# Moving a rarely used branch to the end of a planned three-stage kernel, with its FFN weights split in place and its planner's numbers renewed

## The chip, the core and the metric

The kernel runs on one core of a Trainium2 chip, in one launch. The metric is the device time of that launch in microseconds; the median of several runs counts. A core has five engines that each run their own list of instructions in order: TensorE (PE, with its weight loads PEld), VectorE (DVE), ScalarE (ACT), GpSimd (POOL) and SyncE (SP). They wait for one another by semaphores. DMAs are issued from the queues of SP, ACT and POOL. An instruction that waits holds up everything behind it on its engine.

## What is computed

Softcap attention, then a feed-forward network with x*sigmoid(1.702x), then a top-1 mixture of eight experts:

```python
scores = cap * tanh(scale * q @ k.T / cap)          # B=4, H=12, S=448, D=64, cap=30
attn   = softmax(scores) @ v
x = attn.transpose(0, 2, 1, 3).reshape(1792, 768)
h = x @ w_in;  x = (h * sigmoid(1.702 * h)) @ w_out  # 768 -> 2048 -> 768
e = argmax(x @ w_gate);  gate = softmax(x @ w_gate)[e];  eom = sigmoid(x @ w_output_gate)[e]
out = gate * eom * (relu(x @ w1[e]) @ w2[e])         # 8 experts, 768 -> 1024 -> 768
```

All is fp32 to the outside. Inside, a factor is split into a high part that TensorE's f32r type holds and the rest (`hi` and `lo`), and a product is made of up to three f32r matmuls: hi·hi, hi·lo, lo·hi. Where that is cheaper, one fp32 matmul is used instead.

## The kernel before

**Attention.** Each batch `b` has 12 heads of 4 chunks of 112 queries. A chunk runs `scores` (two f32r matmuls, L620-621), `tanh` (ACT, L625), `exp` (ACT, L629), then for most heads `p_hi` and `p_lo` (a rounding through `rnd_any`, L471 on ACT or L475 on DVE, and a subtraction through `rest_any`, L479; both write the tile `hl`) and `pv` (three f32r matmuls, L648-650). The first `NPVF` = 12 heads, all of batch 0, skip the split: `pv_f` (L642) is one fp32 matmul. After a pair of heads the result is copied out (`u_cp`), its sums go through a chain of small POOL DMAs (`s_ld`, `s_st`, `r_ld`; names `sm`, `rs`, `r`) and a reciprocal on DVE, and the pair is scaled into `x32` and split into `xh` and `xl`.

**Large caps.** The exponential needs no maximum while the cap is at most 40. For larger caps `wide_attention` (L245) computes attention anew in a plain loop. The test on `wide` stands at L441-443, ahead of everything planned: every engine loads the value and branches. If it ran, each pair of heads takes its `x32` from it, by a DMA on POOL's queue under a condition (`x_wide`, L704-706, `x<-xgen`), 24 in all. The condition is false here, but the instruction stands in POOL's order, and `x_hi` waits for it.

**FFN.** Eight halves (batch by half of 2048) in the order (0,0), (1,0), (1,1), (0,1), (2,0), (2,1), (3,0), (3,1). A half has 14 units of weights: 8 of `w_in` with 18 matmuls each and 6 of `w_out` with 24 (`quantum`, L958-960, tile `fps`). For the first half of each kind the weights come from the input, are put together from two words and stored to `wsp`. Later, `ld` (L766) loads a unit from `wsp` to `wf`, `hi` rounds it to the first half of tile `w` and `lo` subtracts into the second. `wf` has `WFR` = 2 buffers, `w` has `WFB` = 4. After the second half of a batch `route(b)` computes expert and place of each token; its last step are four indirect scatters into `tab` on POOL (L1087), each of which waits for the one before.

**Experts.** 21 slots of up to 128 tokens, with loads under a condition (`w_load`, L1300), splits (`w_split`, tiles `mw` and `w`), `l1` (L1391) and `l2` (L1441).

**What sets the order.** Nothing is left to a scheduler of the compiler. Class `Plan` takes tasks with a cost for each engine that may run them, a due time and the buffers they take (`Ring`), simulates them and emits the instructions of each engine in the order in which its list put them. Due times come from constants by stage (`W1`, `AO1`, `CV0`, `SLOT`, ...) less a lead by name (`LEAD`). A transfer costs `bytes / DMAR` on SP's queue and lands `DMAL` later. A task that takes a ring's buffer waits in the plan until the users of the buffer `n` places back are done, and, in `Plan.run` (L174-175), until the first user of the buffer just before it in the ring is done too:

```python
if not r.free and b.at:
    need.add(r.declared[b.at - 1].users[0])
```

For a load that second rule means that the load before has landed. On the chip the order decides, not the planner's times: a semaphore is waited for where the data needs it.

## Time and profile before

| | us |
|---|---|
| median of 3 runs | 1212.81 (1212.13 to 1213.75) |
| profiled execution, its own time | 1217.32 |
| span of its trace | 1215.7 |
| PE / DVE / ACT / POOL busy | 1113.6 / 944.9 / 824.4 / 397.4 |
| mean granted clock of TensorE | 0.976 |

The profile is one execution, 4.5 us over the median; its span lies 1.6 us under its own time. A busy PE is one with matmuls in its array, and their ends are modelled, so sums over a stretch can be compared and single ends cannot. The stretches: attention of batch 0 alone up to 70.3 us; eight FFN halves with the attention of the next batches in between up to 822.1 (the third half ends at 414.6, the first part of the fourth at 448.6, its w_out part at 505.0); experts to the end. A window row gives an engine's busy time in such a stretch, a wait row names what an engine's next instruction waited for last, a timeline row one instruction with the idle time ahead of it.

### The profile page before, as it was taken

The page shows a single profiled execution, that of the slowest core. Times are in us where ns is not written, and L with a number is a line of the kernel's source. Part 1 is how long each engine was busy: PE and PEld are TensorE (multiplying, and loading weights), DVE is VectorE, ACT ScalarE, POOL GpSimd, SP SyncE. Part 2 cuts the span into 40 slices and gives each one's busy share as a digit, 9 for nine tenths or more (in the row PEclk, how much of TensorE's full clock was granted, in tenths as well). Part 3 has the DMA queues.
Part 4 walks back from the last instruction along what each step waited for, and adds up shares of the span by engine and source line. Part 5 has one row for each costly group of instructions (what it writes and reads, how often), then busy time and mean ns, then how long its engine had stood idle before and what let it go on. Part 6 is the DMA issues. An engine that isn't in the chain of part 4 may idle for free.

```text
span 1215.7 us, 16715 instructions
## 1 busy us (share of the span) xinstructions
PE 1113.6 (92%) x5410; PEld 930.5 (77%) x5410; DVE 944.9 (78%) x1461; ACT 824.4 (68%) x1365; POOL 397.4 (33%) x313
## 2 busy tenths in 40 slices
PE   6988898699989995999999998897899999999997
PEld 2446676587777884888888887785788899899897
DVE  4789898688898464578688554558998989999885
ACT  6988798586887422357887332336588888788784
POOL 0222211131141121242132311104575565665651
PEclk9999999899999997999999999999899999999999
DMA  6974667777886574276452374713037951137720
GB/s 166 232 198 136 185 178 201 211 220 212 262 261 187 156 122 82 85 120 147 117 128 81 97 124 89 277 36 111 27 118 283 375 188 40 54 130 260 267 93 31
DMA packets 70218, 191.09 MB, mean 157 GB/s; under 512 B 11362, under 2 KB 21870, under 8 KB 70128
## 3 DMA queue, kind: packets, MB, share of 16 engines
q1 hardware_dynamic: 63440, 170.62, 49.4%
q0 software_dynamic: 6464, 19.16, 5.1%
q8 instruction: 43, 0.70, 0.2%
q14 instruction: 47, 0.39, 0.1%
q10 hardware_dynamic: 224, 0.23, 0.1%
HBM read 244.33 MB, written 28.91 MB: 225 GB/s over the span
## 4 chain that ended last, share of the span: by engine, by line
PE 38%; DMA 10%; DVE 10%; issue 6%; POOL 3%; ACT 2%; SPq 0%; POOLq 0%; DVEq 0%; ACTq 0%
PE hps L1391 8%; PE ops L1441 8%; DMA wf<-wsp 5%; PE fps L958 5%; PE fps L959 5%; PE fps L960 5%; DMA tab<-tokid,posi 2%; DVE w L479 2%; DMA xg<-x2s,gi 1%; DVE mw L479 1%; POOL mw L479 1%; POOL w L479 1%; PE gtp L1409 1%; PE xtp L1361 1%; PE tp L1033 1%
## 5 line engine op out<-in xcount | busy, mean ns | idle before, releaser
L958 PE MATMUL fps<-xh,w 128*128 128x448 f32 x384 | 144.8, 377 | 6.3 <-DVE th L982 6.3
L958 PE MATMUL fps<-gh,w 128*128 128x448 f32 x384 | 144.4, 376 | 5.6 <-ACT acc L1002 3.8
L959 PE MATMUL fps<-gl,w 128*128 128x448 f32 x384 | 142.8, 372 | 3.7 <-DVE gl L479 3.7
L959 PE MATMUL fps<-xl,w 128*128 128x448 f32 x384 | 142.9, 372 | 0.4 <-DVE xl L479 0.4
L960 PE MATMUL fps<-xh,w 128*128 128x448 f32 x384 | 142.7, 372 | 0.0
L960 PE MATMUL fps<-gh,w 128*128 128x448 f32 x384 | 142.3, 370 | 0.0
L629 ACT ACTIVATE p<-p,capa 112x448 f32<-112x448 f32 x192 | 126.4, 667 | 2.6
L479 DVE TENSOR_TENSOR w<-wf,w 128x1024 fp32r<-128x1024 f32 (+3 forms) x95 | 90.6, 959 | 41.3 <-ACT w L471 41.0
L625 ACT ACTIVATE p<-sps 112x448 f32<-112x448 f32 x184 | 97.7, 534 | 19.4 <-PE sps L621 18.0
L471 ACT ACTIVATE w<-wf 128x1024 fp32r<-128x1024 f32 (+3 forms) x75 | 63.9, 851 | 62.5 <-DMA wf<-wsp 33.5
L1441 PE MATMUL ops<-mw,gT 128*128 128x384 f32 x540 | 104.6, 344 | 0.0
L479 DVE TENSOR_TENSOR hl<-p,hl 112x448 fp32r<-112x448 f32 x134 | 95.4, 715 | 11.0 <-ACT hl L471 10.1
L479 POOL TENSOR_TENSOR w<-wf,w 128x768 fp32r<-128x768 f32 (+2 forms) x31 | 63.1, 2035 | 119.7 <-DVE w L475 63.1
L1391 PE MATMUL hps<-mw,xT 128*128 128x512 f32 x390 | 100.4, 409 | 0.0
L479 POOL TENSOR_TENSOR mw<-w1r,mw 128x1024 fp32r<-128x1024 f32 x24 | 76.3, 3193 | 64.0 <-ACT mw L471 63.9
L1441 PEld LDWEIGHTS ops<-mw,gT 128*128 128x128 f32 x540 | 95.8, 192 | 0.9
L471 ACT ACTIVATE mw<-w2r 128x768 fp32r<-128x768 f32 x90 | 75.4, 847 | 30.0 <-PE hps L1391 25.6
L620 PE MATMUL sps<-qks 128*112 128x448 f32 x184 | 79.5, 432 | 14.1 <-ACT vf L471 11.7
L479 DVE TENSOR_TENSOR mw<-w2r,mw 128x768 fp32r<-128x768 f32 x82 | 88.8, 1127 | 0.2 <-ACT mw L471 0.2
L1391 PEld LDWEIGHTS hps<-mw,xT 128*128 128x128 f32 x390 | 74.4, 194 | 16.7 <-ACT h L1404 0.2
L958 PEld LDWEIGHTS fps<-xh,w 128*128 128x128 f32 x384 | 73.5, 191 | 17.6 <-DVE th L982 7.3
L650 PE MATMUL pv<-hl,vs 112*65 112x448 f32 x144 | 55.9, 388 | 33.9 <-DVE hl L479 29.8
(232 smaller groups left out, 2711.4 us busy)
## 6 DMA issues: line engine op xcount, KB each, us to landing
w1r<-in_w_dram SPq DMA_DIRECT2D x60, 1024.0 KB
w2r<-in_w_dram SPq DMA_DIRECT2D x80, 768.0 KB
wf<-wsp SPq DMA_DIRECT2D x56, 384.0 KB
wf<-wsp SPq DMA_DIRECT2D x42, 512.0 KB
qkr<-in_qk_dram SPq DMA_DIRECT2D x95, 224.0 KB
wr<-in_w_in_dram SPq DMA_DIRECT2D x32, 384.0 KB
wr<-in_w_out_dram SPq DMA_DIRECT2D x24, 512.0 KB
x2s<-x2tok SPq DMA_DIRECT2D x4, 1358.0 KB
```

The costliest lines, as they stand in the source:

```text
L471: nc.scalar.activation(o, i, AF.Copy)
L479: e.tensor_tensor(out=o, in0=x, in1=f32(hi), op=ALU.subtract)
L620: mm(sps, lhsT=t[:, 1, sl], rhs=t[:, 0, :], start=True, stop=False)
L625: nc.scalar.activation(p, T["s", kc], AF.Tanh, scale=sct2[:CK] if qkf else 1.0)
L629: nc.scalar.activation(p, p, AF.Exp, scale=capa[:CK])
L650: mm(o, lhsT=VSh[:, 0, c, :], rhs=t[:, 1, :], start=False, stop=c == NC4 - 1)
L958: mm(fps, lhsT=wh, rhs=xh, start=c == 0, stop=False)
L959: mm(fps, lhsT=wh, rhs=xl, start=False, stop=False)
L960: mm(fps, lhsT=wl, rhs=xh, start=False, stop=c == n - 1)
L1033: nc.tensor.transpose(tp[:, j, :], T["x2", u][:, j * CK:(j + 1) * CK], ident)
L1391: mm(T["h", s][n], lhsT=x_[:, kk, :], rhs=w[:, a, n * 512:(n + 1) * 512], start=st_, stop=sp_)
L1441: mm(T["o", s][:, n, :384], lhsT=x_[:, k, :], rhs=w[:, a, n * 384:(n + 1) * 384], start=st_, stop=sp_)
```

## The change

Seven things are done at once.

1. The whole planned body becomes a function `program(ctx, general)`. It is called once with `general=False`, without a test ahead of it. After its end each engine loads `wide` and branches; for a large cap `wide_attention` and a second copy of the program, `program(True)`, which loads `x32` from `xgen`, would overwrite the output. The 24 conditional DMAs go. `exp` is scaled by `capx` = min(cap, 40), so that the first pass stays finite.
2. In the plan, the buffer just before in a ring need only have been started (`first`), not finished.
3. Transfer costs: `DMAR` 330e3 to 300e3, `DMAL` 2.6 to 4.5, POOL's issue 1.1 to 0.6, the small POOL DMAs with landings `SLAT` = (2.8, 4.6, 5.8). The scatters keep theirs, a landing of 2.0.
4. For halves after the first, `ld` loads into the second half of `w` itself, `hi` rounds it into the first and `lo` subtracts in place. `wf` is left to the first half. The load's due time goes from 4 to `WPRE` = 14 ahead.
5. `HB` (buffers of `hl`) 4 to 3, `UB` (of `u`) 2 to 3, `NPVF` 12 to 20: the first eight heads of batch 1 use one fp32 matmul too.
6. The temporary tiles of the index constants at the start share one buffer.
7. All leads and stage constants have other values. They set the order and nothing else.

```diff
-HB = 4
-UB = 2
+HB = 3
+UB = 3
-NPVF = 12
+NPVF = 20
-DMAR = 330e3
-DMAL = 2.6
+DMAR = 300e3
+DMAL = 4.5
-DMAP = 1.1
+DMAP = 0.6
+WPRE = 14.0
+SLAT = (2.8, 4.6, 5.8)
-W1 = 117.691
+W1 = 117.952
...
-                if not r.free and b.at:
-                    need.add(r.declared[b.at - 1].users[0])
+            first = {r.declared[b.at - 1].users[0] for r, b in ((b.ring, b) for b in t.takes) if not r.free and b.at} - need
+            need |= first
...
-                at = max((x.end + self.hop(x, e) for x in t.need), default=0.0)
+                at = max((x.start if x in t.first else x.end + self.hop(x, e) for x in t.need), default=0.0)
...
+    capx = const.tile([128, 1], F32, name="capx")
+    nc.vector.tensor_scalar(out=capx, in0=capa, scalar1=CAPMAX, scalar2=None, op0=ALU.min)
...
-        ti = const.tile([p, n], I32, name=name + "_i")
+        ti = const.tile([128, 32], I32, tag="iota", name=name + "_i")[:p, :n]
...
-    is_wide = nc.values_load(wide[0:1, 0:1], min_val=0, max_val=1)
-    with tc.If(is_wide == 1):
-        wide_attention(tc, nc, qk, v, sct, ncapa, ident, xg)
+    def program(ctx, general):
...
+            if general:
+                for h in range(1, H, 2):
...
+                        nc.sync.dma_start(T["x32", kp], xg[kp[0] * NPAIR + kp[1]].rearrange("a d s -> (a d) s"))
...
-                    nc.scalar.activation(p, p, AF.Exp, scale=capa[:CK])
+                        nc.scalar.activation(p, p, AF.Exp, scale=capx[:CK])
...
-            def x_wide(e, kp=kp):
-                nc.gpsimd.dma_start(T["x32", kp], xg[kp[0] * NPAIR + kp[1]].rearrange("a d s -> (a d) s"),
-                                  cond=is_wide == 1)
-            cc, l = pdma()
-            x = add(cc, s_ld, vc - STG, [xu, u_even], [ub, smb], lat=l)
+                x = add(one("POOL", DMAP), s_ld, vc - STG, [xu, u_even], [ub, smb], lat=SLAT[0])
...
-            x = add(one("POOL", 0.3), x_wide, vc - 6 * STG, [x0, x1], [x32b], lat=0.5)
+                x_split(b, kp, x1, x32b, vc, [x0])
...
-        wb, wfb = r_w.new(), r_wf.new()
+            wb = wbuf[u] = r_w.new()
+            wfb = None if j else r_wf.new()
...
-                T["wf", u] = fr.tile([128, 1024], U32, tag="wf", name="wf")
-                nc.sync.dma_start(T["wf", u][:, :m], wsp[wid][:, :m])
+                    T["w", u] = fw.tile([128, 2, 1024], F32R, tag="w", name="w")
+                    nc.sync.dma_start(T["w", u].bitcast(U32)[:, 1, :m], wsp[wid][:, :m])
...
-                rnd_any(T["w", u][:, 0, :m], f32(T["wf", u][:, :m]), e)
+                    rnd_any(T["w", u][:, 0, :m], f32(T["w", u][:, 1, :m]), e)
...
-                rest_any(T["w", u][:, 1, :m], f32(T["wf", u][:, :m]), T["w", u][:, 0, :m], e)
+                    t = T["w", u]
+                    rest_any(t[:, 1, :m], f32(t[:, 1, :m]), t[:, 0, :m], e)
...
-            x = add(c, ld, vw - 4, stored[wid], [wfb], lat=l)
-            x = add(c_rnd(m), hi, vw, [x], [wfb, wb])
-            wdone[u] = [x, add(c_rest(m), lo, vw, [x], [wfb, wb])]
+                x = add(c, ld, vw - WPRE, stored[wid], [wb], lat=l)
+                x = add(c_rnd(m), hi, vw, [x], [wb])
+                wdone[u] = [x, add(c_rest(m), lo, vw, [x], [wb])]
...
+    with ExitStack() as stack:
+        program(stack, False)
+
+    is_wide = nc.values_load(wide[0:1, 0:1], min_val=0, max_val=1)
+    with tc.If(is_wide == 1):
+        wide_attention(tc, nc, qk, v, sct, ncapa, ident, xg)
+        with ExitStack() as stack:
+            program(stack, True)
```

Lines move: what was L471, L475, L479 and L357 is L476, L480, L484 and L361 after the change; L1087 is L1099, L766 is L778, L1300 is L1312.

**POOL at route(1).** Before, from the first of the four scatters on:

```order
L1087 DMA tab<-tokid,posi 14336x1
L479 TENSOR_TENSOR w<-wf,w 128x768
L1087 DMA tab<-tokid,posi 14336x1 x3
L705 REGISTER_ALU
L705 ISA
L705 DMA x_4777<-xgen 128x448
L693 DMA r<-rs 64x896
L681 DMA sm<-u 128x1x7
L479 TENSOR_TENSOR hl<-p,hl 112x448
L705 REGISTER_ALU
```

After, the same place:

```order
L484 TENSOR_TENSOR w<-w 128x768
L1099 DMA tab<-tokid,posi 14336x1
L705 DMA rs<-sm 128x7
L1099 DMA tab<-tokid,posi 14336x1 x2
L361 TENSOR_SCALAR w<-w 128x768
L1099 DMA tab<-tokid,posi 14336x1
L484 TENSOR_TENSOR qks<-qkr,qks 128x448
L484 TENSOR_TENSOR vs<-vr,vs 112x4x64
L709 DMA r<-rs 64x896
L484 TENSOR_TENSOR w<-w 128x1024
```

The conditional transfers are gone. A rounding of a `w` (the first `w_out` unit of the fourth half) and the chain of a pair's sums now stand among the scatters.

**SP in the w_in part of the last half.** `wf` or `w` from `wsp` are FFN weights, `w1r` and `w2r` weights of the first expert slot. Before:

```order
L1300 DMA w1r_7626<-in_w_dram 128x2x1024
L766 DMA wf<-wsp 128x768
L1300 ISA
L1300 DMA w1r_7655<-in_w_dram 128x2x1024
L1300 ISA
L1300 DMA w1r_7673<-in_w_dram 128x2x1024
L766 DMA wf<-wsp 128x768
L1300 ISA
L1300 DMA w2r_7705<-in_w_dram 128x2x768
L1300 ISA
L1300 DMA w2r_7717<-in_w_dram 128x2x768
L766 DMA wf<-wsp 128x1024 x6
```

After:

```order
L1312 DMA w1r_7294<-in_w_dram 128x2x1024
L778 DMA w<-wsp 128x768
L1312 ISA
L1312 DMA w1r_7331<-in_w_dram 128x2x1024
L778 DMA w<-wsp 128x1024
L1312 ISA
L1312 DMA w1r_7366<-in_w_dram 128x2x1024
L778 DMA w<-wsp 128x1024
L1312 ISA
L1312 DMA w2r_7398<-in_w_dram 128x2x768
L778 DMA w<-wsp 128x1024
L1312 ISA
```

The loads for the experts stood two together between single FFN loads; now each is followed by one FFN load.

**DVE in the attention of batch 1**, in the heads that now use one fp32 product. Before:

```order
L479 TENSOR_TENSOR qks<-qkr,qks 128x448
L479 TENSOR_TENSOR hl<-p,hl 112x448
L475 CAST hl<-p 112x448
L479 TENSOR_TENSOR hl<-p,hl 112x448
L475 CAST hl<-p 112x448
L479 TENSOR_TENSOR hl<-p,hl 112x448
L475 CAST hl<-p 112x448
L671 COPY u<-pv 65x448
L479 TENSOR_TENSOR hl<-p,hl 112x448
```

After:

```order
L484 TENSOR_TENSOR w<-wf,w 128x384
L594 SCALAR_TENSOR_TENSOR qks<-qkr,sct,qks 64x448
L484 TENSOR_TENSOR qks<-qkr,qks 128x448
L687 COPY u<-pv 65x448
L994 SCALAR_TENSOR_TENSOR th<-th,fps 128x448
L480 CAST gh<-th 128x448
L852 TENSOR_SCALAR wg<-wr 128x384
L484 TENSOR_TENSOR gl<-th,gh 128x448
L860 SCALAR_TENSOR_TENSOR we<-we,wg 128x384
L829 SCALAR_TENSOR_TENSOR wf<-wr,we 128x384
```

The copies and subtractions into `hl` are gone; the copies of `u` stay or come to DVE, beside FFN work (`th`, `gh`, `gl`) and the making of weights (`wg`, `we`, `wf`).

## Rows read from the trace of the kernel before

**Rows 1.** Page, part 1: engine, busy us (share of the span) x instructions.
```profile
PE 1113.6 (92%) x5410; PEld 930.5 (77%) x5410; DVE 944.9 (78%) x1461; ACT 824.4 (68%) x1365; POOL 397.4 (33%) x313
```

**Rows 2.** Windows: stretch and length, busy us by engine, then granted clock, DMA share, GB/s.
```profile
0.00:70.30 70.30, 53.73 (x158) 24.86 (x159) 44.69 (x115) 54.56 (x108) 12.19 (x37) 1.00 0.73 191
70.30:329.40 259.10, 224.12 (x998) 174.07 (x997) 225.18 (x421) 206.34 (x404) 52.39 (x70) 0.95 0.71 202
...
448.60:505.00 56.40, 42.55 (x195) 34.44 (x196) 29.81 (x48) 16.03 (x28) 10.12 (x16) 0.85 0.48 80
...
461.20:478.20 17.00, 7.71 (x19) 4.45 (x20) 8.82 (x14) 5.29 (x10) 4.06 (x7) 0.50 0.48 47
...
505.00:682.50 177.50, 174.61 (x876) 149.43 (x875) 133.85 (x225) 124.28 (x225) 53.71 (x51) 1.00 0.48 114
682.50:785.60 103.10, 94.21 (x464) 84.22 (x463) 53.41 (x109) 31.82 (x53) 19.51 (x14) 0.98 0.62 156
...
895.00:1215.70 320.70, 313.13 (x1675) 282.31 (x1673) 282.27 (x272) 255.12 (x334) 174.22 (x81) 1.00 0.48 172
```

**Rows 3.** Waits of PE, 0 to 448.6 us: for what, total us, times, longest.
```profile
PE pv L650 <- DVE hl L479: 23.0, 15, 6.8
PE sps L620 <- ACT vf L471: 11.7, 1, 11.7
```

**Rows 4.** Line L1087 (the scatters): min/median/max ns of issue, first and last start; landing.
```profile
L1087 POOL DMA_INDIRECT tab<-tokid,posi x16: 936/976/1755, 432.4 to 853.2; - x16
...
DMA to landing us min/median/max: 4.5/7.8/10.7
```

**Rows 5.** Timeline around the hole: start, us, engine line operation [idle before <-releaser].
```profile
464.49 0.94 POOL L1087 DMA_INDIRECT tab<-tokid,posi  x1 [9.50 <-DMA tab<-tokid,posi]
464.65 0.04 POOL L705 DMA_DIRECT2D x<-xgen  x1
...
464.69 0.58 ACT L471 ACTIVATE xh<-x 128x448 fp32r<-128x448 f32 x1 [10.59 <-DMA x<-xgen]
...
465.79 0.64 PE L648 MATMUL pv<-hl,vs 112*65 112x448 f32 x1 [5.82 <-ACT hl L471]
...
474.27 0.64 PE L650 MATMUL pv<-hl,vs 112*65 112x448 f32 x1 [3.75 <-DVE hl L479]
```

**Rows 6.** Timeline of the start.
```profile
4.29 0.20 ACT L401 ACTIVATE epst<-ncapa 128x1 f32<-128x1 f32 x1 [1.86 <-DVE wide L399]
...
5.12 0.53 ACTq L548 DMA_DIRECT2D qkr<-in_qk_dram  x1
...
6.08 0.57 SPq L548 DMA_DIRECT2D qkr<-in_qk_dram  x1
```

**Rows 7.** Groups by line: count | busy us, mean ns | idle before, releasers.
```profile
L479 DVE TENSOR_TENSOR hl<-p,hl 112x448 fp32r<-112x448 f32 x134 | 95.4, 715 | 11.0 <-ACT hl L471 10.1
...
L471 ACT ACTIVATE hl<-p 112x448 fp32r<-112x448 f32 x125 | 71.4, 574 | 2.1
...
L671 DVE COPY u<-pv 65x448 f32<-65x448 f32 x12 | 7.1, 594 | 0.0
```

**Rows 8.** Timeline of PE: two fp32 products, one, and f32r matmuls.
```profile
49.10 1.67 PE L642 MATMUL pv<-p,vf 112*65 112x448 f32 x4
51.01 0.92 PE L642 MATMUL pv<-p,vf 112*65 112x448 f32 x2
...
70.47 0.37 PE L958 MATMUL fps<-xh,w 128*128 128x448 f32 x1
70.67 0.37 PE L959 MATMUL fps<-xl,w 128*128 128x448 f32 x1
```

**Rows 9.** Timeline of ACT at 743 us.
```profile
743.32 0.84 ACT L471 ACTIVATE w<-wf 128x768 fp32r<-128x768 f32 x1 [10.06 <-DMA wf<-wsp]
```

**Rows 10.** DMA issues: queue, count, KB each, median us to landing.
```profile
r<-rs POOLq DMA_DIRECT2D x24, 224.0 KB, 5.1
```

**Rows 11.** Waits, 682.5 to 785.6 us.
```profile
ACT w L471 <- DMA wf<-wsp: 27.2, 7, 10.1
```

More of the change, by code (lines that the diff above doesn't have):

```diff
@@ L736, in tile_softcap_attention_ffn_moe @@
-    halves = ([(0, 0), (1, 0), (1, 1), (0, 1)] if SPLIT else [(b, hf) for b in range(2) for hf in range(2)]) + [(b, hf) for b in range(2, B) for hf in range(2)]
-    units = [(b, hf, k, i) for b, hf in halves for k, m in (("a", 8), ("b", 6)) for i in range(m)]
-    NU = len(units) // len(halves)
-    firsts = {hf: next(j for j, x in enumerate(halves) if x[1] == hf) for hf in range(2)}
-    r_wr, r_we, r_wg, r_wf, r_w = Ring(2), Ring(2), Ring(1), Ring(WFR), Ring(WFB)
-    r_th, r_x2 = Ring(2), Ring(2)
@@ L1150, in tile_softcap_attention_ffn_moe @@
-    c, l = dma(0.5e6)
-    x = add(c, lambda e: nc.sync.dma_start(wg32, w_g.rearrange("(k p) e -> p k e", p=128)), WGV, lat=l)
-    x = add(one("POOL", 0.25, True), lambda e: rnd_pool(wgs[:, :, :16], wg32), WGV, [x])
-    add(one("DVE", 0.17, True), lambda e: rest(wgs[:, :, 16:], wg32, wgs[:, :, :16]), WGV, [x])
-    add(one("SP", 0.3), lambda e: nc.sync.dma_start(tab.rearrange("(p a) b -> p (a b)", p=128), zer), WGV)
-    for b in range(B):
-        attention(b)
-        if b == 1 and SPLIT:
-            xagain = [r.new() for r in r_x]
```

1824 lines of the change are left out of this document (923 added, 901 removed).

## Prediction

> **What bounds the kernel now.** I read the page first, then the windows by stage, then the waits inside the stages that lose. By the page TensorE is busy 92% of the span, DVE 78%, ACT 68% and POOL 33% [rows 1]. The share is a mean over unlike stages, so the windows come next [rows 2]. From 895 us to the end, the steady part of the mixture of experts, PE is busy 313.1 of 320.7 us: nothing done to other engines can gain there. Up to 329.4 us three engines share the load: PE has 53.7 + 224.1 = 277.8 us of 329.4, DVE 44.7 + 225.2 = 269.9, ACT 54.6 + 206.3 = 260.9, and PE waits for what DVE has late. From 448.6 to 505.0 PE has 42.55 of 56.4 us, and inside it, 461.2 to 478.2, only 7.71 of 17.0 at a granted clock of 0.50, the lower of its two levels. From 682.5 to 785.6 it has 94.2 of 103.1. The waits of PE up to 448.6 say what is late: 23.0 us in 15 waits for `hl` on DVE (the low half of the probabilities), and 11.7 us once, at the start [rows 3].
>
> The hole at 461 us is read in order of time. The four indirect scatters of a `route` each wait for the one before to land. They took 4.5 to 10.7 us, median 7.8 [rows 4]. The last of route(1) sat 9.50 us and left POOL at 464.49; behind it stood the conditional `x<-xgen`, issued at 464.65. ACT's `xh<-x` had waited 10.59 us for that transfer and started at 464.69; PE's `pv` waited 5.82 us for ACT's `hl`, which stood behind `xh` on ACT, and another `pv` waited 3.75 us for `hl` at 474.27 [rows 5].
>
> **The change part by part.** The profiled run took 1217.32 us with a span of 1215.7; the median of the runs is 1212.81. I add differences of the span to the median.
>
> *Start and end.* The test for large caps no longer stands ahead of the loads. The first score matmul needs two halves of `qkr`. Ahead of the test ACT's last operation is `epst` (0.20 us from 4.29), for which it waited for the test's value on DVE; then ACT issues its half at 5.12 and SP the other at 6.08 [rows 6]. After the change SP's comes first on its queue; ACT's half still stands behind `epst`, so the later issue moves from 6.08 to about 4.5: -1.6 us (between -0.6, ACT's own move, and -3 if the landings ahead of it also quicken). The test now runs at the end on every engine. At the start 1.8 us lie between 4.29 and SP's half, part of it taken by another load, so the cost is between 0 (beside the landing of the last output) and +1.8; I take +1.0. The second program that follows is never entered.
>
> *Single products for 8 more heads.* 32 chunks of batch 1 lose one `p_hi`, one `p_lo` and three matmuls, and get one fp32 matmul instead. ACT rounds 125 of the 144 such chunks and DVE subtracts in 134 of 144, so 32 chunks free 32 x 125/144 x 0.574 = 16 us of ACT and 32 x 134/144 x 0.715 = 21 us of DVE [rows 7]. The order gives DVE 16 more copies of `u`, 16 x 0.594 = 9.5 us, which leave ACT. DVE is left with about -12, less some splits of weights that the new order gives it. On PE two fp32 products in a row take 1.67 us against 0.92 for one, so 0.75 each; f32r matmuls start 0.20 apart, so three are 0.61 [rows 8]. That is 32 x 0.14 = +4.5 us of PE, hidden in the 51.6 us that PE idles up to 329.4; without that cover it costs all 4.5. What it gains on the path is bounded by PE's wait for `hl`: 32 of the 96 chunks of batches 1 and 2 that run up to 448.6 are a third of 23.0 = 7.7 us; all ACT relief together (16 + 9.5 = 25.5 us of ACT, which is 79% busy there) could give up to 20; if PE's addition isn't hidden and something else is late at the same places, 0. I take -10, nearest to the row of waits. What is late next is `qks` and the splits of weights on the same DVE.
>
> *The hole at 448.6 to 505.* Three things that made it leave: the 24 conditional transfers on POOL go (each stood behind a scatter or a chain, and ACT's in-order queue behind it); the 20 heads with single products and new due times spread attention of batch 2 over all stages up to 448.6, where before it was issued early; and the hi/lo work of the last chunks isn't queued behind `xh`. Without the hole, the 42.55 busy us stay, less about half of the 7.71 that ran at the lower clock: 38.7 us. The gain is 56.4 - 38.7 = 17.7 us (0 if another wait takes its place, 20 if the stage also sheds its last pieces).
>
> *New work behind scatters.* The planner still reckons a scatter at 2.0 us, and its order now puts other things between them. On POOL a `w` rounding, the high half of the first unit of w_out of the fourth half, stands behind the third scatter of route(1). In the profile a scatter follows the last by about 10.5 us (9.50 of wait and 0.94 of its own), so the rounding starts some 21 us after the first scatter, at 432.4, and the weights are ready about 23 us after it. PE wanted them 448.6 - 432.4 = 16 us after it. That is a stall of 7 us, less what PE has more to do there (attention of batch 2 and the fp32 products). Route(0) has a similar place with `v_hi`. Both together: between 0 and +15, taken as +6. DVE's subtraction and PE's unit are queued behind that rounding; the row loads `r<-rs` behind the fourth scatter are due later.
>
> *Loads in place.* Weights of the halves after the first are loaded into the second half of `w` itself. A load had to wait for DVE's subtraction two units back; now it waits until PE has finished the unit four back, so the lead is three units: 3 x 18 x 0.20 = 11 us where a unit has 18 matmuls, 3 x 24 x 0.20 = 14.7 us with 24 [rows 8]. Before, the two `wf` tiles stood in addition to the four `w` tiles, so a load could be up to five units ahead. A load and two splits have to fit in 11 us; ACT's rounding takes 0.84 [rows 9] and I estimate the subtraction at 1.0, so the load has 9.2. The nearest rows: a 224 KB load from POOL lands after 5.1 us [rows 10], and one 384 KB `wf` kept ACT idle 10.06 us [rows 9]. So most fit and those beside heavy traffic do not. Before, ACT waited 27.2 us for `wf` in 7 waits between 682.5 and 785.6 [rows 11], where PE lost 8.9 us. In the new order the expert loads of 1 MB are interleaved one to one with these loads, not four together, which speaks for a gain there; the shorter lead for a loss. Between -9 and +15; I take 0. That SP's queue now stands on PE's progress is the part that I trust least: `qkr` and `vr` loads of attention are queued behind a waiting `w` load.
>
> *Experts.* Fewer splits on POOL and some more on DVE, beside a busy PE: 0, between -4 and +4 for the stretch ahead of 895.
>
> *Ring rule, transfer times.* They change only the order; their effect is in the terms above.
>
> Sum: -1.6 + 1.0 - 10 - 17.7 + 6 + 0 + 0 = -22.3, so 1212.8 - 22.3 = **1190.5 us**.
>
> A rule of the Trainium skill speaks to two of these terms. The scatters land after a median of 7.8 us [rows 4]. By the page "DMA: Bandwidth & Descriptors", section "Anatomy of one DMA — SWDGE (gpsimd) path", a transfer from this path costs about 2.0 us plus its bytes at 436 GB/s, so a scatter of a few hundred bytes would take about 2.0, as the planner says, and an estimate by that formula for a 384 KB load is 2.9 us. The trace disagrees for both kinds that it shows, 7.8 for the scatter and 5.1 for 224 KB. By the page the sixth term would be 0 and the sum 1184.5.
>
> **The rivals.** *Everything fits* (quick transfers): scatters land at their shortest, 4.5 us, so that the third leaves about 11 us after the first and the rounding is ready before the 16 us are up; and no weight load takes over 9.2 us, so the 8.9 us lost before 785.6 come back. Then -22.3 - 6 - 8.9 gives 1175.6. For it: the interleaved loads and the unloaded POOL queue. Against it: the median of 7.8. The page's formula would be this case.
>
> *The hole moves.* The scatters still take over 40 us in a chain, and each thing queued behind them waits. The stall at the start of the w_out part is the full 7, that of route(0) 8, and half of the hole stays (9). Then -1.6 + 1 - 10 - 9 + 15 = -4.6 at worst, and with the middle of the stalls about -10: 1203.
>
> *Slower: the weight loads bound.* One mechanism: with three units of lead a load that needs over 9.2 us from PE's release to landing stalls PE by what it is over, and the next one is released late by as much, so nothing catches up. There are 98 such loads; each 0.45 us over on average costs 44 us, and the result is 1190.5 + 44 = 1234. It decides from an average of 0.23 us a load (22.3/98). For it: 10.06 us in the profile, SP in order behind waits on PE. Against it: 505 to 682.5 has PE busy 174.6 of 177.5 us [rows 2] in a kernel with the same bytes, and the 10 us load stood in the time of scatters and of a burst.
>
> *The change doesn't do what it says*: the hole's place is taken over by PE's own order and the time stays within 0.2%.
>
> **How the numbers follow.** Forecast 0.47 (1180 to 1200), everything fits 0.18 (1175), the hole moves 0.17 (1203, of which 0.02 lands within 0.2% of before), weight loads bound 0.14 (1215 to 1240), no change 0.04. A measurement of this kernel tells 0.2%, 2.4 us. Faster is 0.47 + 0.18 + 0.15 = 0.80, same 0.06, slower 0.14. The range goes from 1168, a little under the fast rival, to 1213, where the slow one begins: it leaves out the slow rival and some 0.04 below.
>
> **What would show it.** Right: the first score matmul near 10 us; PE's wait for `hl` up to the fourth half under 16 us; no stretch at clock 0.50 of over 10 us between 400 and 500; that part of the fourth half near 39 us. The stall behind scatters shows as PE or DVE waiting for a `w` from POOL at the first w_out unit of the fourth half. Wrong: ACT or DVE waiting for `w<-wsp` by DMA in most units, SP's queue mostly waiting on PE, with PE gaps of one to three us at each unit in the last halves; or the steady part from 895 on longer than 320.7 us.

## The result, and the profile after

The changed kernel takes 1172.37 us in the median (four runs, 1170.34 to 1177.73), the kernel before 1213.28. The ratio is 0.9664, with a 95% interval of 0.9624 to 0.9703. The span of the profiled run is 1171.1 us, 44.6 less than before.

The page of the kernel after, part 1 and the PE rows of part 2 (busy time in 40 slices, and the granted clock); part 1 answers to [rows 1]:

```profile
PE 1099.8 (94%) x5378; PEld 925.9 (79%) x5378; DVE 903.7 (77%) x1467; ACT 800.7 (68%) x1302; POOL 323.0 (28%) x275
...
PE   5989999999989779989999999987999999999996
...
PEclk9999999999999979989999999998999999999999
```

PE is busy 94% of a shorter span, with 14 us less of busy time (part of it had run at the lower clock); POOL lost 74 us, DVE 41, ACT 24. Besides the first slice, PE dips at 381 to 439 us (7 and 7 tenths, the clock 7 tenths in the second) and at 761 to 820.

Windows of the kernel after, in stages as in [rows 2], each from the first matmul of a part to the next (columns as there; the number in brackets behind an engine's busy time counts its instructions). The first row is the kernel before, up to its third half:

```profile
0.00:329.40 329.40, 277.84 (x1154) 198.94 (x1155) 269.87 (x534) 260.90 (x512) 64.58 (x107) 0.96 0.71 200
...
0.00:280.40 280.40, 257.88 (x1072) 184.22 (x1073) 234.51 (x475) 223.06 (x431) 53.05 (x85) 0.99 0.76 215
...
371.30:422.60 51.30, 40.77 (x208) 35.12 (x207) 30.67 (x67) 21.39 (x40) 12.43 (x11) 0.90 0.60 109
422.60:463.50 40.90, 36.81 (x178) 32.53 (x178) 25.42 (x36) 16.03 (x25) 9.17 (x9) 0.92 0.37 118
...
644.30:775.70 131.40, 128.02 (x655) 114.55 (x653) 73.13 (x141) 48.69 (x76) 15.04 (x11) 1.00 0.52 140
...
846.00:1171.10 325.10, 315.21 (x1689) 286.06 (x1687) 264.07 (x291) 258.26 (x335) 118.98 (x67) 0.99 0.47 171
```

Up to the third half, which begins at 280.4 us and began at 329.4, PE is busy 257.9 us and idles 22.5; before it was busy 277.8 and idled 51.6. That is where the gain is: PE idles 29.1 us less up to there, and over the whole span 30.8 less (102.1 before, 71.3 after). The w_in and w_out parts of the fourth half, 371.3 to 463.5, have PE busy 77.6 of 92.2 us: the loss there is as large as it was. The last four parts, 644.3 to 775.7, take 131.4 us, 139.6 before, and the experts start at 775.7, 822.1 before. From there on nothing is gained: 395.4 us against 393.6.

| begin of (us in the trace) | before | after | difference |
|---|---|---|---|
| first score matmul | 11.8 | 12.4 | +0.6 |
| second half | 223.9 | 202.5 | -21.4 |
| third half | 329.4 | 280.4 | -49.0 |
| fourth half | 414.6 | 371.3 | -43.3 |
| its w_out part | 448.6 | 422.6 | -26.0 |
| fifth half | 505.0 | 463.5 | -41.5 |
| seventh half | 682.5 | 644.3 | -38.2 |
| experts | 822.1 | 775.7 | -46.4 |
| end | 1215.7 | 1171.1 | -44.6 |

The -49.0 at the third half is not all gain. 1154 matmuls stood ahead of that point, now 1072. The single products account for 32 of the 82 (the trace counts an fp32 product as two matmuls, so a chunk has two instead of three); the other 50 are attention that now runs later. PE's idle time ahead of the point tells more than its place.

Waits of PE up to 422.6 us in the kernel after, which answer to [rows 3]:

```profile
PE sps L636 <- ACT vf L476: 12.4, 1, 12.4
PE fps L970 <- DVE th L994: 10.7, 2, 10.4
...
PE pv L666 <- DVE hl L484: 1.3, 1, 1.3
```

The wait for `hl` fell from 23.0 us to 1.3. A new one of 10.4 us stands in its place, for DVE's `th`.

**The new gap, read in order of time.** Timeline of the kernel after around 400 us, on POOL, then DVE, ACT and SP's queue:

```profile
407.02 0.96 POOL L1099 DMA_INDIRECT tab<-tokid,posi  x1 [8.38 <-DMA tab<-tokid,posi]
408.02 0.84 POOL L361 TENSOR_SCALAR w<-w 128x768 fp32r<-128x768 f32 x1
414.47 1.02 POOL L1099 DMA_INDIRECT tab<-tokid,posi  x1 [5.61 <-DMA tab<-tokid,posi]
415.52 1.16 POOL L484 TENSOR_TENSOR qks<-qkr,qks 128x448 fp32r<-128x448 f32 x1
...
408.89 0.96 DVE L484 TENSOR_TENSOR w<-w 128x768 fp32r<-128x768 f32 x1 [13.35 <-POOL w L361]
...
412.08 0.61 DVE L994 SCALAR_TENSOR_TENSOR th<-th,fps 128x448 f32<-128x448 f32 x1
...
412.73 0.58 ACT L476 ACTIVATE gh<-th 128x448 fp32r<-128x448 f32 x1 [11.17 <-DVE th L994]
...
426.72 1.06 ACT L476 ACTIVATE w<-w 128x1024 fp32r<-128x1024 f32 x1 [6.79 <-DMA w<-wsp]
...
416.71 1.11 SPq L564 DMA_DIRECT2D qkr<-in_qk_dram  x2
417.91 5.43 SPq L778 DMA_DIRECT2D w<-wsp  x3
```

The third scatter of route(1) waited 8.38 us for the second and was issued at 407.02. Behind it stood the rounding of `w` at 408.02. DVE's subtraction of that unit waited 13.35 us for it; DVE's `th`, which waited for nothing but its place, came at 412.08, and ACT's `gh` had waited 11.17 us for that. PE idled from 402.5 to 412.8. The second gap, 426.7 to 430.8, is ACT's `w`, which waited 6.79 us for a load: SP issued an attention load (`qkr`) at 416.71 and only then, at 417.91, the weight load behind it. The `qkr` load in turn waited until POOL had read the tile, at 415.52, behind the fourth scatter.

**Start.** Timeline of the kernel after, the rows that answer to [rows 6]:

```profile
0.79 0.58 SPq L564 DMA_DIRECT2D qkr<-in_qk_dram  x1
...
4.70 0.15 DVE L394 TENSOR_SCALAR ncap<-capt 128x1 f32<-128x1 f32 x1 [3.66 <-DMA capt<-in_cap_dram]
...
5.72 0.20 ACT L407 ACTIVATE epst<-ncapa 128x1 f32<-128x1 f32 x1 [3.42 <-DVE ncapa L401]
5.73 0.53 ACTq L564 DMA_DIRECT2D qkr<-in_qk_dram  x1
...
10.83 0.67 ACT L579 ACTIVATE qks<-qkr,sct 128x448 fp32r<-128x448 f32 x1 [4.91 <-DMA qkr<-in_qk_dram]
...
12.37 0.69 PE L636 MATMUL sps<-qks 128*112 128x448 f32 x1 [12.37 <-ACT vf L476]
```

SP's loads do come first now, at 0.79. But DVE's first operation on the cap waited 3.66 us for the cap's 512 bytes, which were now under way beside them, and ran at 4.70 (3.27 before). So `epst` ran at 5.72 (4.29 before), ACT's half of `qkr` was issued at 5.73 (5.12 before) and landed at 10.83, and PE began 0.6 us later.

### The profile page after: what moved, and what is told of

It is laid out like the page before. It is cut to its first block, busy times and chain, and to the rows that moved or that the text cites. A ratio compares the mean times of both kernels' runs of the same rounds, so it can differ in the third digit from the quotient of the medians.

```text
span 1171.1 us, 16399 instructions
## 1 busy us (share of the span) xinstructions
PE 1099.8 (94%) x5378; PEld 925.9 (79%) x5378; DVE 903.7 (77%) x1467; ACT 800.7 (68%) x1302; POOL 323.0 (28%) x275
## 4 chain that ended last, share of the span: by engine, by line
PE 54%; DVE 5%; DMA 5%; issue 4%; POOL 2%; ACT 0%; SPq 0%; POOLq 0%; DVEq 0%
PE ops L1453 13%; PE hps L1403 12%; PE fps L970 7%; PE fps L971 7%; PE fps L972 7%; DMA w<-wsp 2%; DMA tab<-tokid,posi 2%; PE gtp L1421 1%; DVE mw L484 1%; POOL tab L1099 1%; PE xtp L1373 1%; PE tp L1045 1%; PE sps L637 1%; PE sps L636 1%; PE pv L664 1%
## 5 line engine op out<-in xcount | busy, mean ns | idle before, releaser
L645 ACT ACTIVATE p<-p,capx 112x448 f32<-112x448 f32 x192 | 126.0, 671 | 3.0
L484 DVE TENSOR_TENSOR w<-w 128x768 fp32r<-128x768 f32 (+1 forms) x80 | 86.1, 1077 | 51.7 <-ACT w L476 37.7
L636 PE MATMUL sps<-qks 128*112 128x448 f32 x184 | 84.3, 458 | 15.1 <-ACT vf L476 12.4
L1403 PE MATMUL hps<-mw,xT 128*128 128x512 f32 x390 | 96.8, 402 | 0.3 <-ACT h L1416 0.3
L476 ACT ACTIVATE mw<-w2r 128x768 fp32r<-128x768 f32 x89 | 74.6, 846 | 30.3 <-PE hps L1403 22.4
L476 ACT ACTIVATE w<-w 128x768 fp32r<-128x768 f32 (+1 forms) x68 | 63.0, 929 | 45.4 <-DMA w<-wsp 45.4
L484 DVE TENSOR_TENSOR mw<-w2r,mw 128x768 fp32r<-128x768 f32 x81 | 80.6, 1017 | 12.1 <-ACT mw L476 11.6
L1403 PE MATMUL hps<-w,xT 128*128 128x512 f32 x330 | 82.0, 398 | 8.2 <-POOL w L484 5.2
L970 PEld LDWEIGHTS fps<-gh,w 128*128 128x128 f32 x384 | 72.8, 190 | 15.9 <-DVE th L994 4.5
L1453 PE MATMUL ops<-w,gT 128*128 128x384 f32 x420 | 82.0, 343 | 1.0 <-ACT y L1460 1.0
L484 DVE TENSOR_TENSOR hl<-p,hl 112x448 fp32r<-112x448 f32 x105 | 69.1, 660 | 16.0 <-ACT hl L476 15.6
```

The costliest lines, as they stand in the source:

```text
L476: nc.scalar.activation(o, i, AF.Copy)
L484: e.tensor_tensor(out=o, in0=x, in1=f32(hi), op=ALU.subtract)
L636: mm(sps, lhsT=t[:, 1, sl], rhs=t[:, 0, :], start=True, stop=False)
L645: nc.scalar.activation(p, p, AF.Exp, scale=capx[:CK])
L970: mm(fps, lhsT=wh, rhs=xh, start=c == 0, stop=False)
L1403: mm(T["h", s][n], lhsT=x_[:, kk, :], rhs=w[:, a, n * 512:(n + 1) * 512], start=st_, stop=sp_)
```

## The experiments

Ratios are to the kernel before, run beside them (1220.1 to 1220.8 us there); after is 0.9664, from the runs in which the kernel before took 1213.28. Two ratios differ by more than chance from about 0.006, or 7 us. Spans and stages are from each kernel's profiled run. Those of one order repeat well up to the third half: it starts at 278.7 to 282.4 us in the kernel after and in the five versions that keep its order there. Where the planner orders anew, an edit moves things all over the program, so each is read by stages.

### One rounding off POOL

```diff
         for t in order:
+            if t.fn.__name__ == 'hi' and (t.fn.__defaults__ or (0,))[0] == 48:
+                t.eng = 'DVE'
             t.fn(t.eng)
```

> The kernel after the change, its order of instructions kept, with one rounding (the high half of FFN unit 48, the seventh w_in unit of the fourth half) on DVE instead of POOL, where it stands behind the third scatter of route(1). If that queue position is what stops DVE for 13.4 us and PE for 10.85 us at 402 us, both waits go; the gap of 4.66 us at 426 us is a knock-on (DVE's work for attention behind the stopped subtraction, SP's weight load behind an attention load that waits for it) and goes too: 1172 becomes 1157 to 1161. Rival: the load of unit 48 or the scatters' traffic is late as well, or the gap moves on to the next thing behind the scatters: 1167 or more.

Measured: 0.9653 (0.9611 to 0.9695), span 1172.1. The rival holds. The w_in part fell from 51.3 to 43.7 us, and the w_out part rose from 40.9 to 51.1. POOL, SP and ACT of this kernel at that place:

```profile
414.98 1.01 POOL L1101 DMA_INDIRECT tab<-tokid,posi  x1 [7.24 <-DMA tab<-tokid,posi]
416.01 1.16 POOL L486 TENSOR_TENSOR qks<-qkr,qks 128x448 fp32r<-128x448 f32 x1
...
417.19 1.11 SPq L566 DMA_DIRECT2D qkr<-in_qk_dram  x2
418.40 1.48 SPq L780 DMA_DIRECT2D w<-wsp  x3
...
428.06 1.06 ACT L478 ACTIVATE w<-w 128x1024 fp32r<-128x1024 f32 x1 [15.45 <-DMA w<-wsp]
```

Behind the fourth scatter POOL has the low half of a key (`qks`, 416.01). SP's load of the next key waits until that tile is read, and behind it on SP's queue are the weights of units 51 on; ACT waited 15.45 us for the first. The gap of PE, 13.2 us from 418.9, is the old one, one link further on.

### Everything computed by POOL behind the scatters moved to DVE

```diff
+        tail = 0
         for t in order:
+            if t.eng == "POOL" and t.fn.__name__ == "<lambda>" and ".route." in t.fn.__qualname__:
+                tail = 3
+            elif tail and t.eng == "POOL" and "DVE" in t.cost:
+                t.eng = "DVE"
+                tail -= 1
             t.fn(t.eng)
```

> The kernel after the change, order kept, with every compute task that POOL has between a route's first scatter and the third one after its fourth moved to DVE at its place in the plan (at route(1): the rounding of unit 48, the key's low half of head 1 of the last batch, its value's low half). With the rounding alone moved, the gap went on to SP: its key load waited for that low half behind the fourth scatter, and the weights of unit 51 behind it came 15.5 us late. If POOL's queue behind the scatters is the whole cause, both gaps (10.9 and 4.7 us) go, the w_in and w_out parts of the fourth half take 40 and 36 us (51.4 and 40.8), and the ratio to before falls from 0.966 to 0.952 to 0.957. Rival: what is left behind the scatters on POOL (sums and row loads) or the loads themselves keep the gap: 0.962 to 0.968.

The edit moves up to three such tasks behind each scatter. Measured: 0.9552 (0.9509 to 0.9595), span 1159.8. The two parts take 45.0 and 38.1 us, 9.1 less together though more than the 40 and 36 expected, and the part after them, with route(0) in it, 43.8 instead of 50.3. Gaps of 5.3 us at 411.0 and 2.1 at 422.0 are left. The experts start 13.9 us earlier and take 2.6 longer. So POOL's queue behind the scatters cost the kernel after some 14 us, by the trace as by the ratio (0.0112 x 1220 = 13.7).

### The 24 conditional transfers taken out of the kernel before

```diff
-            x = add(one("POOL", 0.3), x_wide, vc - 6 * STG, [x0, x1], [x32b], lat=0.5)
+            x, also = x1, [x0]
```

(`x_st` and `x_hi` depend on `[x] + also`.)

> The kernel before, without the 24 conditional transfers on POOL, so a large cap would be computed wrongly; the test at the start stays, the planner orders anew. If these transfers made the hole at 461 us, the w_out part of the fourth half (56.4 us) takes 47 or less, and the whole 8 to 15 us less. Rival: the row loads and sums of the same pairs stand behind the scatters as well and hold up x just as long: that part stays over 52 us and the time within 4 us.

Measured: 1.011 (1.0067 to 1.0153), span 1224.2, the part 57.5 us (56.4 before). The rival holds for the part. It doesn't for the time, which rose by 13 us, not by at most 4: the edit only takes work away, but the planner's new order is worse, up to the third half already (335.5 against 329.4). A new order alone can thus cost 13 us, and every run below in which the planner orders anew carries such a doubt. POOL, PE and DVE of this kernel:

```profile
472.26 0.94 POOL L1087 DMA_INDIRECT tab<-tokid,posi  x1 [9.34 <-DMA tab<-tokid,posi]
473.20 0.59 POOL L693 DMA_DIRECT2D r<-rs  x1
473.81 1.13 POOL L479 TENSOR_TENSOR gl<-th,gh 128x448 fp32r<-128x448 f32 x1
...
474.99 0.74 PE L959 MATMUL fps<-gl,w 128*128 128x448 f32 x1 [9.90 <-POOL gl L479]
...
481.41 0.62 DVE L699 TENSOR_TENSOR x<-u,r 64x448 f32<-64x448 f32 x1 [13.18 <-DMA r<-rs]
```

Without the transfers a row load and a `gl` stand right behind the fourth scatter. PE waited 9.90 us for the one and DVE 13.18 for the other. What is queued there changes with the order; in both traces something that other engines need is, and PE stands.

### 12 heads on single products, as before

```diff
-NPVF = 20
+NPVF = 12
```

> The kernel after the change with 12 heads on single fp32 products as before, not 20; the planner orders everything anew. If the 8 heads' worth of splits that went is what closed the gaps of PE between 63 and 240 us (48.7 us of lost time there before, 10.2 after), these come back in good part: the third half starts 25 us or more later than at 280 us. Rival: the new order (ring rule, transfer times, due times) closed them: the third half starts less than 12 us later, of which a few are work.

Measured: 0.9669 (0.9628 to 0.971), span 1183.9. The third half starts at 291.2 us, 9 to 12 us after that of every version with the order of after. Up to there PE idles 31.0 us, 8.5 more, and its waits for `hl` are 6.1 us (1.3 after). The rival holds: most of the gain there is not the heads'. In the whole the ratio shows 0.6 us, give or take 7, so little of the 10 may be left at the end; the profiled run was the longest of four (1185.6, the others 1179.3 to 1182.9).

### Separate buffers for loaded weights

```diff
-            wfb = None if j else r_wf.new()
+            wfb = r_wf.new()
-                    T["w", u] = fw.tile([128, 2, 1024], F32R, tag="w", name="w")
-                    nc.sync.dma_start(T["w", u].bitcast(U32)[:, 1, :m], wsp[wid][:, :m])
+                    T["wf", u] = fr.tile([128, 1024], U32, tag="wf", name="wf")
+                    nc.sync.dma_start(T["wf", u][:, :m], wsp[wid][:, :m])
...
-                x = add(c, ld, vw - WPRE, stored[wid], [wb], lat=l)
+                x = add(c, ld, vw - WPRE, stored[wid], [wfb], lat=l)
```

> The kernel after the change with the FFN weights of later halves loaded into separate buffers (two, as before) ahead of the four w buffers; the planner orders anew. If loading in place costs lead (three units instead of five), this is faster by 3 to 8 us in the last two halves, where ACT waits 18.9 us for such loads. If the lead of three units is enough, the stretch of the last four stages (131.4 us) stays within 2 us, and the time moves only as the new order lets it, within 6 us.

Measured: 0.9708 (0.9666 to 0.9751), 5 us more by the ratio, which may be chance, span 1182.5. The last four parts take 136.7 us, 5.3 more than with loads in place (131.4, and 131.7 to 132.7 in the five versions with its order): a loss where the first expectation had a gain, and beyond the 2 us of the second. Waits of SP's weight loads (L778) in this kernel and in the kernel after, over the whole program:

```profile
SPq L778 <- DVE w L484: 153.0, 50, 6.7
...
SPq L778 <- POOL w L484: 94.4, 20, 21.2
...
SPq L778 <- PE fps L972: 268.2, 67, 8.4
```

With separate buffers a load waits mostly for the subtraction, on DVE or on POOL, once 21.2 us. In place it waits for PE in all but one case, never longer than 8.4 us. The longer lead of five units exists only if the subtractions are early.

### The due times of before

```diff
-LEAD = {'tanh': -0.33, 'v_hi': 0.96, ...
+LEAD = {'tanh': -0.21, 'v_hi': 3.06, ...
-W2 = 199.014
+W2 = 252.95
-SLOT = 17.742
+SLOT = 17.468
...
```

> The kernel after the change with all due times and leads of before (LEAD, the stage constants, CV0, CV1, SLOT and the like); ring rule, transfer times, buffers, heads and in-place loads stay. With 12 single heads the stretch up to the third half grew only from 280 to 291 us, against 329 before, so some 38 us come from the order. If the due times make it, the third half starts at 305 us or later here; if the ring rule and the transfer times make it, before 295 us.

Measured: 0.9734 (0.9694 to 0.9774), span 1182.9. The third half starts at 292.8, 12.4 later, but 49 more matmuls stand ahead of it; PE idles 22.7 us up to there, as after (22.5). The experts start at 774.3, 1.4 earlier, and take 408.6 us instead of 395.4: that is where the time is lost. So the FFN and attention part gains as much with the old due times.

### The ring rule of before, and the transfer numbers of before

```diff
-                at = max((x.start if x in t.first else x.end + self.hop(x, e) for x in t.need), default=0.0)
+                at = max((x.end + self.hop(x, e) for x in t.need), default=0.0)
```

> The kernel after the change, but in the plan a ring's task waits again for the end of the first user of the buffer just before it (for a load: for its landing); all else as after, order anew. Old due times cost only 12 us up to the third half and 12 single heads 11, of 49 us that this stretch gained. If the ring rule makes most of the rest, the third half starts at 300 us or later (280 after, 329 before). Rival: the rule changes the plan little, since a load's landing is far ahead of its use in any case: below 288 us.

Measured: 1.0372 (1.0331 to 1.0414), span 1256.7. The third half starts at 312.7, 32.3 later, but 80 more matmuls stand ahead of it, and PE idles 31.3 us up to there, 8.8 more. Most of the loss comes behind: over the whole span PE idles 128.3 us instead of 71.3, and it is busy 28.6 us more at a mean granted clock of 0.962 instead of 0.982.

```diff
-DMAR = 300e3
-DMAL = 4.5
-DMAP = 0.6
-SLAT = (2.8, 4.6, 5.8)
+DMAR = 330e3
+DMAL = 2.6
+DMAP = 1.1
+SLAT = (2.6, 2.6, 2.6)
```

> The kernel after the change with the planner's transfer numbers of before (330 GB/s and 2.6 us on SP, POOL's issue 1.1, its small transfers landing 2.6 later); all else as after, order anew. If it is the transfer times that put loads early enough, the third half starts at 295 us or later. Rival: the lead of 14 ahead of the weights' due time and the ring rule do that already: below 288 us.

Measured: 1.0002 (0.997 to 1.0035), span 1223.7. The third half starts at 305.2, 24.8 later, with as many matmuls ahead of it, and PE idles 38.6 us up to there, 16.1 more. The experts start at 824.5.

Windows up to the third half: with the old due times, the old ring rule, the old transfer numbers, and with the two new ones alone in the kernel before (the next experiment):

```profile
0.00:292.80 292.80, 270.06 (x1121) 191.65 (x1122) 247.30 (x499) 244.02 (x470) 59.26 (x96) 0.99 0.79 219
...
0.00:312.70 312.70, 281.38 (x1152) 194.04 (x1153) 248.57 (x490) 255.74 (x499) 68.97 (x102) 0.99 0.70 201
...
0.00:305.20 305.20, 266.64 (x1071) 188.83 (x1072) 233.16 (x468) 223.55 (x433) 63.02 (x95) 0.96 0.73 204
...
0.00:313.70 313.70, 273.63 (x1153) 193.84 (x1154) 266.22 (x529) 258.69 (x504) 78.08 (x118) 0.99 0.73 208
```

Each of these two takes away the whole gain or more. Neither brings back PE's waits for `hl` up to the third half (23.7 us before; 2.5 with the old rule, none with the old numbers): PE waits for other things there. Where the first loses most, its PE waits over the whole span show, and POOL's timeline beside the longest:

```profile
PE fps L972 <- POOL w L484: 32.6, 6, 16.7
...
455.94 0.94 POOL L1099 DMA_INDIRECT tab<-tokid,posi  x1 [8.41 <-DMA tab<-tokid,posi]
456.90 1.81 POOL L484 TENSOR_TENSOR w<-w 128x768 fp32r<-128x768 f32 x1
```

PE waited 32.6 us, 16.7 at a stretch, for subtractions on POOL; the longest stood behind the fourth scatter. So at least part of the 86 us isn't the price of the rule itself: the order that it leads to has worse places in it.

### The ring rule and the transfer numbers alone, in the kernel before

```diff
-                if not r.free and b.at:
-                    need.add(r.declared[b.at - 1].users[0])
+            first = {r.declared[b.at - 1].users[0] for r, b in ((b.ring, b) for b in t.takes) if not r.free and b.at} - need
+            need |= first
...
-DMAR = 330e3
-DMAL = 2.6
-DMAP = 1.1
+DMAR = 300e3
+DMAL = 4.5
+DMAP = 0.6
```

> The kernel before with two of the seven parts alone: the new ring rule and the new transfer times; heads, buffers, due times, wf buffers, the test at the start and the conditional transfers as before. If these two make most of the gain in attention whatever the due times are, the third half starts at 305 us or earlier (329 before) and the whole is 15 us or more below before. Rival: they need the other parts (in-place loads, heads, due times): within 8 us of before.

Measured: 1.0046 (1.0021 to 1.0072), span 1228.9. The third half starts at 313.7, 15.7 earlier with as many matmuls ahead of it, and not at 305; PE idles 40.1 us up to there, 11.5 less, and waits 13.2 us for `hl` instead of 23.7. The fourth starts 14.9 earlier, and all of it is lost again by the experts (826.6, 4.5 later), which take 402.3 us. The rival holds for the whole: alone these two, with the other parts' constants as before, are worth nothing.

### The start

```diff
-                    (nc.scalar if k == (0, 0) and a else nc.sync).dma_start(t[a * D:(a + 1) * D], qk[k[0], k[1]])
+                    nc.sync.dma_start(t[a * D:(a + 1) * D], qk[k[0], k[1]])
```

> The kernel after the change with both halves of the first qkr load on SP's queue, none on ACT's. If the start is set by ACT's half, which stands behind ACT's exponential of the cap (issued 5.73 us, landed 10.8), the first score matmul moves from 12.4 us to about 8 and the whole to 1168. Rival: the start's gain is lost again in attention of batch 0, where ACT sets the pace, or the second load on SP holds up the ones behind it: 1171 to 1174.

Measured: 0.9644 (0.9599 to 0.969), span 1180.7 (the longest of its four runs). The first score matmul came at 11.1, not 8. I put that down to DVE's copy of a value tile, which stood ahead of the key's split; but the copy ran at 9.82 without a wait, 0.46 us long, and up to there DVE was busy with the index constants. The interval holds both expectations of the time.

With this, and POOL's tasks moved, the two copies were put later:

```diff
+        later("v_f", (0, 0), "k_lo", (0, 0))
+        later("v_f", (0, 1), "exp", (0, 0, 0))
         for t in order:
```

> The one before, and the start eased: both halves of the first qkr load on SP, and the two first value copies, which wait for later loads, moved behind the first key split on DVE and the first exponential on ACT. With only the load moved, PE began at 11.1 us, since DVE's value copy waited till 9.8. If in-order queues are what is left, the first score matmul comes at 7 to 8 us and the whole is 3 to 4 us below the run before (0.949 to 0.953). Rival: PE begins early but attention of batch 0 is set by ACT's and DMA's pace: less than 1.5 us below.

Measured: 0.9569 (0.951 to 0.9627), span 1160.6, no gain over 0.9552. The first score matmul came at 10.8. Timeline of its start:

```profile
6.82 0.16 DVE L448 CAST pref<-pref_i 128x8 f32<-128x8 int32 x1
7.05 0.13 POOL L447 IOTA ebase_i<- 128x8 int32 x1 [0.30 <-DVE pref L448]
7.22 0.17 DVE L448 CAST ebase<-ebase_i 128x8 f32<-128x8 int32 x1 [0.24 <-POOL ebase_i L447]
...
9.71 0.20 DVE L448 CAST tokid<-tokid_i 112x16 f32<-112x16 int32 x1 [0.24 <-POOL tokid_i L447]
...
9.94 0.68 DVE L608 SCALAR_TENSOR_TENSOR qks<-qkr,sct,qks 64x448 fp32r<-64x448 f32 x1
```

DVE and POOL take turns on the one shared tile, an index constant each 0.41 us, from 6.82 to 9.94; each waits until the other has written or read it. The key's split stands behind the last.

```diff
-        ti = const.tile([128, 32], I32, tag="iota", name=name + "_i")[:p, :n]
+        ti = const.tile([p, n], I32, name=name + "_i")
```

> The run with POOL's tasks moved from behind the scatters and the start eased, and each index constant at the start back in its own temporary tile. With the shared tile POOL and DVE took turns from 6.7 to 9.9 us (one waits until the other has written or read), and DVE's first key split began only at 9.94. If that is what held the start at 10.8 us, the first score matmul comes before 8.5 us and the whole is 2 to 3 us below (0.951 to 0.954). Rival: attention of batch 0 is bound by ACT or by loads: the first part of the first half starts at 62 to 63 us as before, the whole within 1 us.

Measured: 0.9512 (0.9475 to 0.9548), span 1154.4. The last of those rows and PE's first now:

```profile
7.72 0.68 DVE L608 SCALAR_TENSOR_TENSOR qks<-qkr,sct,qks 64x448 fp32r<-64x448 f32 x1
...
8.55 0.69 PE L650 MATMUL sps<-qks 128*112 128x448 f32 x1 [8.55 <-DVE qks L608]
```

The first score matmul is at 8.55 and the first half starts at 59.5 (63.0 with the shared tile). Of the 6 us between the spans the start explains 3.5; by the ratios alone (0.9569 and 0.9512) the step isn't told from chance. The version as a whole is faster than both kernels: its interval lies below that of the change (0.9475 to 0.9548 against 0.9624 to 0.9703), some 18 us.

## Why the prediction was right, and where it was not

The time, 1172.4, is in the range, and faster was right. The forecast of 1190.5 was 18 us too slow; the time is nearest the rival in which everything fits (1175.6), but only in part for that rival's reason: of the 9.2 us that PE lost in the last four parts 5.8 came back, but the scatters were not quick. That the forecast came this near is partly chance. The hole and the stalls together were to give -11.7 and gave +1.8 (the two parts took 90.4 us and take 92.2); the order, which had no term, gave more than was missing there.

| term | forecast | measured | by |
|---|---|---|---|
| start | -1.6 | +0.6 | first score matmul, trace after |
| end | +1.0 | +2.4 | last matmul to end of span: 5.5 before, 7.9 after |
| single products | -10 | -8.5 of PE's idle time up to the third half; 0 to 7 in the end | 12 heads |
| hole | -17.7 | the parts 371.3 to 463.5 idle 14.6; 15.0 before | windows |
| new work behind scatters | +6 | some 14, 9 of it in the two parts of the row above | POOL's tasks moved |
| loads in place | 0 | -8.2 in the last four parts; 5.3 less of it with separate buffers | windows |
| ring rule, transfer times | none of their own | of PE's -29.1 of idle time up to the third half: -11.5 alone in the kernel before; +8.8 and +16.1 when one is undone | windows |

**Single products: right where they act.** A third of PE's wait for `hl`, 7.7 us, was a fair row to go by: with 12 heads 4.8 us of that wait come back, and 8.5 of idle time. The added PE work doesn't show (busy 260.2 us up to the third half with 12 heads, 257.9 with 20). That the gain would last to the end isn't shown.

**Ring rule and transfer times: the step that failed.** "They change only the order; their effect is in the terms above" is true in its first half. In its second it made the effect of the order that of the parts I could see in it. PE's idle time up to the third half fell from 51.6 us to 22.5, and the heads explain 8.5 us of that. The old transfer numbers bring back 16.1, the old ring rule 8.8, the old due times 0.2. I had the row for this in hand: 51.6 us of idle PE while PE is 84%, DVE 82% and ACT 79% busy is a stretch where the order, not an engine, is short, and I bounded the gain there by one wait.

How far each of the two carries it can't be said: they don't add up. Alone in the kernel before they took 11.5 us of idle time ahead of the third half, nearly all of it waits for `hl`, and lost them later; with either taken from the kernel after the whole gain is gone, but by other waits. Of the 22.4 us of waits for `hl` that went, the runs thus show some 10 for these two and 5 for the heads; no run undid the numbers of buffers of `hl` and `u`. The due times were worth nothing by the experts, and 13 us in them. I leave open which share is better knowledge of transfers and which is that the constants suit this set of rules.

**The hole: right place, wrong cause.** That the scatters' chain is behind it was right. "Three things that made it leave", the conditional transfers first among them, fell: without them the part took 57.5 us. They happened to be what stood behind the fourth scatter. The second, heads and due times, doesn't make it leave either: over the fourth half PE idles 11.5 us with 12 heads and 18.0 with the old due times, 14.6 in the kernel after. So the hole didn't go; the sum of idle PE in the two parts is 14.6 us, against 1.2 + 13.9 = 15.0 before (34.0 - 32.83 and 56.4 - 42.55). What the part from 448.6 gained, the part ahead of it lost. That part before:

```profile
414.60:448.60 34.00, 32.83 (x176) 29.21 (x175) 21.86 (x46) 11.91 (x22) 12.20 (x8) 1.00 0.60 134
```

In mechanism this is the rival in which the hole moves. Its 1203 was too slow for the same reason as the forecast: it had no term for the order either.

**New work behind scatters: right mechanism, size wrong.** The rounding that I named stopped DVE and PE as described, with scatters 7.5 to 10.4 us apart. I took it for a w_out unit wanted 16 us after the first scatter; unit 48 is the seventh w_in unit and wanted earlier, and the second gap behind it, by SP's queue, I hadn't priced. (In the sum this is the fifth term; the prediction calls it the sixth.) By the page "DMA: Bandwidth & Descriptors" of the Trainium skill (section "Anatomy of one DMA — SWDGE (gpsimd) path") a transfer that POOL's queue issues takes about 2.0 us plus the time of its bytes. The trace after again disagrees; the waits of POOL's scatters (L1099) there, from issue to landing:

```profile
DMA to landing us min/median/max: 4.5/7.9/10.9
```

**Loads in place.** A lead of three units was enough: ACT waits 18.9 us for weights in the last four parts (27.5 before), and PE idles 3.4 us there (9.2 before). The rival of late loads did not come: SP's loads wait 268.2 us for PE, but in the last four parts that costs PE no more than these 3.4. By the one run with separate buffers I had the trade backwards: the five units of lead hung on subtractions that came late. How much of the -8.2 is the loading in place isn't shown; the interleaved loads and the due times changed with it.

**Start.** The later half of `qkr` moved as I said on SP and the other way on ACT: I had let ACT's half hang on `epst` and not followed what `epst` hangs on, the 512 bytes of the cap, now beside some 0.9 MB of other loads (qkr at 224 KB, three times, and vr at 112 KB, twice). The shared tile of the index constants I had dropped as nothing. In the change it is hidden by the late load; with that mended it moves the first matmul by 2.2 us. The end term, too, lay outside the bounds that I gave it, 0 to +1.8.

**The signs.** Of the signs of being right, the waits for `hl` came (1.3 us), and the w_out part is near 39 us (40.9). The first score matmul did not (12.4), and the granted clock stood at 0.50 for 10.2 us from 405.6, ahead of that part. The stall came at a w_in unit. Of the signs of being wrong two came without the loss that they were to show: SP's weight loads wait mostly for PE, and the steady part of the experts takes 325.1 us; the experts as a whole take 1.8 us more than before.

## What to carry to other kernels

An instruction stands behind what its engine's queue waits for, whatever its own inputs: behind a chain of dependent indirect DMAs put nothing that another engine needs, and look one link further after each repair, since a moved task shows the next one in the queue. Where no engine is busy throughout and the gaps are many and short (here PE 84%, DVE 82%, ACT 79% up to the third half), price the order itself, not the work that is removed from it. Compare stages by the idle time ahead of a point, with the instructions counted, since a new order also moves work across it. A planner's constants and rules are one set: two of the parts alone were worth nothing, and with either of them taken out the whole gain was gone.

## What the runs showed of the hardware

A load of 512 bytes issued at 1.08 us on ACT's queue was used at 4.70 with SP's loads beside it, 3.27 (issued at 1.21) without. Two engines that take turns on one small tile need 0.41 us for a pair of operations that take 0.13 and 0.16 us by themselves. And the test at the end shows: the span ends 7.9 to 8.1 us after the last matmul in the eleven traces that have it there, 5.5 to 5.7 in the three that don't. On POOL, the last engine to reach it, loading the value takes 0.31 us; then 2.6 us pass between the branch over the second program and the next instruction:

```profile
L1552 POOLq EVENT_SEMAPHORE  x6: 17/30/43, 1168.5 to 1168.9; - x6
...
L1552 POOLq COMPARE_BRANCH  x1: 45/45/45, 1165.8 to 1165.8; - x1
```

On the other four engines it is 2.6 to 3.9 us. Behind the branch over the short code of the last slot, just ahead, POOL needs 0.2. So most of the difference lies behind the jump over the second program; what passes there the trace doesn't show.
